# Diagonal sums of the last chunk by VectorE in f32, a last output of 320 and 64 columns, and a new order of steps

## The chip, the cores and the metric

The kernel runs on one core of a Trainium2 chip. The metric is device time in microseconds (us) of one execution; a median of several runs is given, and one further execution was taken with the hardware profiler. The engines have short names: PE is TensorE (matmuls; PEld its weight loads), DVE is VectorE, ACT is ScalarE, POOL is GpSimd, SP is SyncE, which here only issues DMA transfers.

## The reference

An RWKV attention with a decaying state, and after it two matmuls with a squared ReLU between them. Cut to what is computed:

```python
# r, k, v: (4, 8, 768, 48) f32; w, u: (8, 48); w_in (384, 2048), w_out (2048, 384)
for t in range(S):
    cur = einsum('bhd,bhe->bhde', u[None] * k_t, v_t)
    y[:, :, t] = einsum('bhd,bhde->bhe', r_t, state + cur)
    state = w[None, :, :, None] * state + einsum('bhd,bhe->bhde', k_t, v_t)
x = y.transpose(0, 2, 1, 3).reshape(B * S, H * D)       # (3072, 384)
h = maximum(x @ w_in, 0.0)
out = (h * h) @ w_out
```

The part with `u` is the diagonal of the attention: token t sees its own v with the weight sum over d of r, u and k. That sum, for each token and head, is "the diagonal sum" below.

## The kernel before

The 768 tokens are cut into 6 chunks of 128, and each chunk of each of the 4 batches is a unit: 24 units, numbered chunk by chunk, so units 20 to 23 are the last chunk. The heads are padded from 48 to 64 and lie in pairs of 128 rows (`HP` = 4 pairs).

For each unit, in short names that are also the keys of the planner:

- `rt`, `kt` (function `load`, on SP) and `vt` (`load_v`, on POOL) bring r, k and v in f32, 192 KB each.
- `scale` (DVE) multiplies r and k by powers of w and casts to bf16 (`rkw`). `rkT` turns them: units 0 to 5 by PE (`turn`) and ACT, all later ones by a transposing DMA of SP (`turn_dma`).
- `at` (8 matmuls) makes the scores of the 8 heads; `mask` (two DVE products) keeps their upper triangle.
- `rk` (DVE) is the bf16 product of the turned r and k; `sums` multiplies it on PE with `uwb`, a block matrix of u, in 4 matmuls of 8 columns: these are the diagonal sums `t["d"]`. Where a next chunk follows, 4 more matmuls of 96 columns make the step of the state (`sadd`, `sdec` on DVE, `stb` on ACT).
- `dv` (DVE) multiplies the sums with v, `y` (8 or 12 matmuls) applies scores and state to v, and `yb` (DVE) adds the two.
- `xT` turns the result: units 0 to 5 by PE and ACT, the others by a transposing DMA of SP (`x_dma`).
- `m1` (function `mm1`): for each of four quarters of `w_in`, 12 matmuls of 128 columns; `relu` (ACT) and `sq` (ACT or DVE) follow.
- `m2` (`mm2`): for each quarter of `w_out`, 4 matmuls of 384 columns, accumulated over the four quarters; `osb` (ACT) empties the bank and `out` (SP) stores 192 KB.

The last unit's output is made in two parts, `PARTS`, of 256 and 128 columns (`mm2_half`): the first part is emptied by ACT and the second by DVE, and each is stored by itself.

The order of all this is written out by hand for each engine: a class `Plan` simulates the engines with a cost for each step and always starts, on a free engine, the ready step of lowest rank. Each step is added with its engine, cost, needs and rank; the table `TURNS` replaces the ranks of single steps. What comes out is one fixed list per engine, which that engine works through in order: a step that waits holds up all behind it on its engine. Where PE has nothing ready in the first 16 us of the plan, it gets a filler matmul (`fill`, L380).

The eight weight quarters (I 0 to I 3 of w_in, O 0 to O 3 of w_out, 128 x 1536 elements each) are loaded by POOL. `FRONT` names for each a `gate`: a tiny POOL copy out of an r or k tile, so that the transfer starts only when that tile has landed. `load_v` has such a gate too: v of a unit waits for k of the unit before.

Lines the text speaks of: L380 filler, L392 spread of the logarithms of w, L436/L438 loads of r and k, L442 gate, L445 and L448 weights, L460/L458 `scale`, L476 transposing DMA of r and k, L487 turn by PE, L513 `rk`, L521 `at`, L533 `mask`, L541 and L546 the two kinds of `sums`, L563 `sdec`, L576 and L582 `y`, L623 `m1`, L647 `m2`, L663 the last output's matmuls, L675 and L679 its copy and store.

Of the kernel before, what the change touches and what calls it, by code (L numbers as in the profile page):

```python
# [9 lines left out]
F32 = mybir.dt.float32  # L10
BF16 = mybir.dt.bfloat16
AF = mybir.ActivationFunctionType
ALU = mybir.AluOpType
# [153 lines left out]
def kernel(  # L167
# [11 lines left out]
    nc = tc.nc  # L179
    B, H, S, D = r.shape  # L180
    C = 128
# [18 lines left out]
        },  # L200
        "O": {
            0: 76.019, 1: 91.228, 2: 107.535, 3: 7
        },
        "rt": {
            0: -83.003, 1: -66.162, 12: 22.377, 13: 28.231, 14: 28.49, 15: 33.657, 3: -36.29, 5: 1.476, 8: 3.237
        },
        "kt": {
            0: -80.584, 1: -55.486, 10: 19.508, 11: 20.529, 2: -47.443, 6: 2.358
        },
        "at": {  # L210
            0: -3.958, 11: 34.671, 4: -16.745, 7: 10.944
        },
        "mask": {
            (1, 0): -39.238, (10, 0): 33.02, (2, 1): 25.375, (5, 1): 1.515
        },
        "sadd": {
            1: 9.124, 4: 45.244
        },
        "rk": {
            2: 13.012, 7: 14.32, 8: 68.867, 9: -12.042  # L220
        },
        "sums": {
            11: 49.353, 2: -24.778, 8: 5.082
        },
        "dv": {
            2: -26.848, 7: 34.164, 9: -12.993
        },
        "stb": {
            2: -9.741, 4: 57.421
        },  # L230
        "scale": {
            (10, 0): 23.594, (11, 0): -15.371, (3, 0): -29.763, (4, 0): 33.082, (7, 1): 6.517, (8, 1): 4.379
# [5 lines left out]
            3: 5.236, 8: 23.726  # L238
# [8 lines left out]
            (4, 0): -1030.12, 12: 30.174, 4: -16.809  # L247
        },
        "y": {
            11: 43.479, 5: 9.48, 6: 18.808, 9: 29.593  # L250
        },
        "sdec": {
            6: 13.634, 8: 4.888, 9: -24.389
        },
        "yb": {
            6: 3.845
        },
        "sq": {
            (0, 1): 18.299, (0, 2): 50.562, (1, 3): 45.386, (2, 2): 48.536, (3, 2): 52.143, (4, 1): 54.301, (9, 2):
            69.323  # L260
        },
        "m1": {
            (0, 2): -16.746, (1, 0): -1.05, (2, 1): -30.817, (3, 0): 10.204, (4, 2): 48.519, (5, 1): 23.695, (5, 2):
            34.027, (7, 1): 57.358, (8, 3): 44.479, (9, 0): 48.671, (9, 2): 56.936, (9, 3): 69.933
        },
        "relu": {
            (0, 2): 29.056, (1, 3): 26.845, (2, 0): -1.314, (3, 0): 53.81, (7, 1): 50.455
        },
        "m2": {
            (1, 1): 27.683, (1, 2): 12.22, (2, 1): 34.668, (2, 3): 24.074, (3, 0): 21.896, (3, 1): 50.716, (3, 3):  # L270
            -14.219, (4, 0): -2.879, (5, 3): 5.654, (6, 1): 66.17, (7, 1): 43.242, (7, 2): 41.92, (8, 0): 93.885
        },
        "I": {
            0: 0, 1: 1, 2: 3, 3: 5
# [7 lines left out]
    PAIRED = ()  # L282

# [91 lines left out]
    gate = const.tile([128, 1], F32)  # L375

# [133 lines left out]
    def rk(i):  # L510
        t = tiles[i]
        t["rk"] = work.tile([128, HP, C], BF16, name="rk")
        nc.vector.tensor_tensor(t["rk"], t["rkT"][:, 0], t["rkT"][:, 1], ALU.mult)  # L513

# [141 lines left out]
    PARTS = (slice(0, 256), slice(256, dm))  # L656
# [36 lines left out]
    def do(fn, *a):  # L693
        return lambda: fn(*a)
# [19 lines left out]
    for n, (what, q, gated) in enumerate(FRONT):  # L714
        copy(
            (what, q), POOL, 1.0, do(weights, gated, q, what), rank=n,
            move=((2.35, 96, 2.8, 0.0, 0.0) if what == "I" else (2.15, 65, 2.8, 0.0, 0.0)), needs=[gated], uses=[gated],
        )
    for i in range(NU):
# [44 lines left out]
        add(("rk", i), DVE, 0.335, do(rk, i), rank=a + 1, needs=[("rkT", i)], new=[("rk", i)], uses=[("rkT", i)])  # L764
# [9 lines left out]
        for o in range(2):  # L774
# [4 lines left out]
        add(  # L779
            ("sums", i), PE, 0.275 if c < NCH - 1 else 0.105, do(sums, i), rank=a + (2.1 if c else 2.1),  # L780
            needs=[("rk", i), "uwb", ("at", i)] + ([("kb", i) if i < NKE else ("scale", i, 1), ("vb", i)] if c < NCH - 1 else []),
            new=[("s", i)], uses=[("rk", i), ("rkw", i)] + ([vb] if c < NCH - 1 else []),
        )
        add(("dv", i), DVE, 0.465, do(diag_v, i), rank=a + 2, needs=[("sums", i), ("vb", i)], new=[("dv", i)], uses=[("s", i), vb])
# [27 lines left out]
    for m in GROUPS:  # L812
# [17 lines left out]
        for j in range(i, i + m):  # L830
# [12 lines left out]
            for n in range(2):  # L843
                add(
                    ("m2", j, n), PE, (1.74, 0.9)[n], do(mm2_half, j, n), rank=a + n + L2,
# [4 lines left out]
                    ("osb", j, n), (ACT, DVE)[n], 0.3, do(evict_half, j, n), rank=a + n + L2 + 0.4, needs=[("m2", j, n)],  # L850
# [4 lines left out]
        rt=7, kt=7, vt=7, rkw=NPAD, g=2, rkT=6, vb=NVB, rk=4, am=8, dv=4, yb=4, xT=3, gr=6, osb=6,  # L855
# [34 lines left out]
```

## Time and profile before

| | us |
|---|---|
| median of 3 runs | 175.74 (175.08 to 176.27) |
| the profiled execution | 176.04 |
| its span, first to last instruction | 174.3 |
| POOL gate copies in front of v (L465), idle until k landed | 80.9 |
| DVE squares (L640), idle until ACT's relu | 21.5 |
| ACT copies of the output (L654), idle until PE | 15.8 |

The span lies within the profiled execution's own time; 1.7 us are around it. Idle time of an engine that nobody waits for costs nothing: the three largest waits in the table belong to engines that others do not wait for at that moment. In the profile's views, rows of groups end with busy time, mean ns of one instruction, idle time before it and what ended it. Rows in order of time begin with start and length in us.

### The profile page before, as it was taken

To read this page: it belongs to the slowest core of one execution; us is meant where nothing else is said; L and a number is where in the kernel's file an instruction comes from. 1 tells how busy PE (TensorE), PEld (TensorE's weight loads), DVE (VectorE), ACT (ScalarE), POOL (GpSimd) and SP (SyncE) were. 2 spreads that over 40 slices of the span, in tenths; PEclk is the share of its full clock that TensorE was granted. 3 is DMA by queue.
4 is the path that set the end of the run, shared out by engine and by line. 5 is a ranking of instruction groups with operands and counts; after the bars stand their busy time and mean duration, and the time that the engine had idled before them with its cause. 6 is when DMAs were issued, how large, how long until landed. Compare 5 with 4: busy or idle time off the path is not lost.

```text
span 174.3 us, 5795 instructions
## 1 busy us (share of the span) xinstructions
PE 166.7 (96%) x2390; PEld 134.7 (77%) x2390; DVE 121.1 (70%) x252; ACT 132.1 (76%) x268; POOL 40.0 (23%) x84
## 2 busy tenths in 40 slices
PE   7978899999999999999999999999999999999991
PEld 6766799887687787886896787869787698877871
DVE  7869976615999899977986799794989635531010
ACT  3946999999458797886968876939994869948640
POOL 7866890300140220302032202203202000000000
PEclk9999999999999999999999999999999999999999
DMA  4889999999999999999999999999999971130121
GB/s 97 228 179 246 232 218 193 185 221 118 170 201 164 178 154 209 200 214 170 231 142 183 156 237 214 218 177 141 186 200 175 271 180 26 26 111 6 47 81 56
DMA packets 76474, 28.93 MB, mean 166 GB/s; under 512 B 65440, under 2 KB 75296, under 8 KB 76448
## 3 DMA queue, kind: packets, MB, share of 16 engines
q1 hardware_dynamic: 70848, 20.56, 69.8%
q0 software_dynamic: 5312, 7.87, 23.9%
q8 instruction: 18, 0.29, 0.8%
q10 hardware_dynamic: 288, 0.15, 0.4%
q14 instruction: 8, 0.07, 0.1%
HBM read 20.50 MB, written 4.72 MB: 145 GB/s over the span
## 4 chain that ended last, share of the span: by engine, by line
PE 81%; DMA 11%; SPq 4%; issue 1%; DVE 0%; POOL 0%; POOLq 0%
PE bank L623 35%; PE bank L647 33%; DMA w_in_q<-in_moe_w_in_dram 5%; SPq L436 4%; DMA rkT<-rkw 4%; PE bank L521 4%; DMA rt<-in_r_dram 2%; PE bank L576 2%; PE bank L582 2%; PE bank L546 2%; PE bank L663 2%; PE bank L541 1%; PE bank L487 0%; PE bank L607 0%; POOL gate L442 0%
## 5 line engine op out<-in xcount | busy, mean ns | idle before, releaser
L623 PE MATMUL bank<-xT,w_in_q 128*128 128x128 bf16 x1152 | 70.7, 219 | 0.1
L623 PEld LDWEIGHTS <-w_in_q 128*128 128x128 bf16 x1152 | 66.5, 98 | 3.1 <-DMA w_in_q<-in_moe_w_in_dram 0.3
L647 PE MATMUL bank<-w_out_q,g 128*128 128x384 bf16 x368 | 66.9, 326 | 0.0
L631 ACT ACTIVATE gr<-bank 128x512 f32<-128x512 f32 x96 | 54.3, 599 | 13.6 <-PE bank L623 13.3
L647 PEld LDWEIGHTS <-g 128*128 128x128 bf16 x368 | 33.3, 98 | 19.8
L638 ACT ACTIVATE g<-gr 128x512 bf16<-128x512 f32 x72 | 43.7, 637 | 0.4
L533 DVE TENSOR_TENSOR am<-bank,smask 128x512 bf16<-128x512 f32 x48 | 31.3, 682 | 3.3 <-PE bank L521 3.1
L640 DVE TENSOR_TENSOR g<-gr 128x512 bf16<-128x512 f32 x24 | 16.5, 686 | 21.5 <-ACT gr L631 21.5
L465 POOL COPY gate<-kt 128x1 f32<-128x1 f32 x22 | 5.8, 266 | 80.9 <-DMA kt<-in_k_dram 80.9
L654 ACT COPY osb<-bank 128x384 f32<-128x384 f32 x23 | 11.0, 483 | 15.8 <-PE bank L647 15.8
L467 POOL DMA_DIRECT2D vt<-in_v_dram x24 | 21.4, 893 | 5.9 <-issue 1.6
L555 DVE TENSOR_TENSOR dv<-vb,bank 128x384 f32<-128x384 bf16 x24 | 13.2, 548 | 5.3 <-PE bank L546 3.4
L513 DVE TENSOR_TENSOR rk<-rkT 128x512 bf16<-128x512 bf16 x24 | 10.0, 417 | 7.7 <-DMA rkT<-rkw 4.3
L591 DVE TENSOR_TENSOR yb<-bank,dv 128x384 bf16<-128x384 f32 x24 | 13.2, 550 | 2.8 <-PE bank L582 2.4
L471 ACT CAST vb<-vt 128x384 bf16<-128x384 f32 x24 | 12.4, 518 | 0.0
L458 DVE TENSOR_TENSOR rkw<-rt,wpos 128x384 bf16<-128x384 f32 x18 | 9.8, 550 | 1.4 <-DMA rt<-in_r_dram 1.4
L458 DVE TENSOR_TENSOR rkw<-kt,wneg 128x384 bf16<-128x384 f32 x18 | 9.9, 549 | 0.9 <-DMA kt<-in_k_dram 0.9
L567 ACT CAST stb<-st 128x384 bf16<-128x384 f32 x20 | 10.4, 519 | 0.0
L380 PE MATMUL bank<-warm 128*128 128x128 bf16 x98 | 9.3, 248 | 1.1 <-DVE warm L322 1.1
L521 PE MATMUL bank<-rkT 64*128 64x128 bf16 x192 | 9.5, 219 | 0.2
L494 ACT COPY rkT<-bank 128x512 bf16<-128x512 bf16 x12 | 6.8, 588 | 3.0 <-PE bank L487 3.0
L563 DVE TENSOR_TENSOR st<-st,wend 128x384 f32<-128x384 f32 x16 | 8.8, 549 | 0.0
(74 smaller groups left out, 129.1 us busy)
## 6 DMA issues: line engine op xcount, KB each, us to landing
vt<-in_v_dram POOLq DMA_DIRECT2D x24, 192.0 KB, 4.6
out_dram<-osb SPq DMA_DIRECT2D x23, 192.0 KB, 4.0
rt<-in_r_dram SPq DMA_DIRECT2D x18, 192.0 KB, 4.5
kt<-in_k_dram SPq DMA_DIRECT2D x18, 192.0 KB, 4.3
w_in_q<-in_moe_w_in_dram POOLq DMA_DIRECT2D x4, 384.0 KB, 7.9
w_out_q<-in_moe_w_out_dram POOLq DMA_DIRECT2D x4, 384.0 KB, 12.7
kt<-in_k_dram SPq DMA_DIRECT2D x12, 96.0 KB, 4.3
rt<-in_r_dram SPq DMA_DIRECT2D x11, 96.0 KB, 4.2
```

What stands on the lines that cost most here:

```text
L458: nc.vector.tensor_tensor(t["rkw"][:, x, :, :, :D], pair(src), pair(wneg if x else wpos), ALU.mult)
L467: nc.gpsimd.dma_start(out=tiles[i]["vt"], in_=v[b, :, c * C : (c + 1) * C, :].rearrange("h s d -> s h d"))
L471: nc.scalar.copy(tiles[i]["vb"], tiles[i]["vt"])
L521: nc.tensor.matmul(out=t["at"][o][:, p, :], lhsT=t["rkT"][sl, 1, p, :], rhs=t["rkT"][sl, 0, p, :], start=True, stop=True,)
L533: nc.vector.tensor_tensor(am, t["at"][o], smask.unsqueeze(1).to_broadcast([C, HP, C]), ALU.mult)
L555: nc.vector.tensor_tensor(t["dv"], t["vb"], t["d"].unsqueeze(2).to_broadcast([C, H, D]), ALU.mult)
L591: nc.vector.tensor_tensor(t["yb"], t["y"], t["dv"].rearrange("p h d -> p (h d)"), ALU.add)
L623: nc.tensor.matmul(out=t["h", s][:, a], lhsT=turned, rhs=chunks[c]["xT"][:, n, b : b + m, :], start=(n == 0), stop=(n == NK - 1),)
L631: nc.scalar.activation(t["gr", s], t["h", s], AF.Relu)
L638: nc.scalar.activation(g, x, AF.Square)
L640: nc.vector.tensor_tensor(g, x, x, ALU.mult)
L647: nc.tensor.matmul(out=t["o"], lhsT=chunks[units[i][0]]["g"][:, f, units[i][1], :], rhs=w_out_q[f // 4][:, f % 4, :], start=(f == 0), stop ...
```

## The change

Four things are changed.

1. For units 20 to 23 (`NDV = 20`) the diagonal sums no longer come from PE. Three DVE instructions make them from the f32 tiles: r times k, times u, and a reduction over the 48 elements of each head. `dv` then reads them from SBUF. The 4 matmuls of 8 columns of each of these units, and the bf16 product before them, are gone. `r` and `k` tiles are read by these steps too.
2. For this u must lie on all 128 partitions: four f32 matmuls of 96 columns in the head spread it (`spread_u`), and DVE copies it to SBUF (`copy_u`).
3. The last output's parts are 320 and 64 columns wide.
4. `TURNS` and `FRONT` are new, and so is the order on every engine.

```diff
@@ functions
+    u_all = const.tile([C, H, D], F32)
+    def spread_u():
+        spread["u"] = bank("h", "u")[:, :dm]
+        for a in range(HP):
+            nc.tensor.matmul(
+                out=spread["u"][:, a * 2 * D : a * 2 * D + 2 * D], lhsT=ident4[:, a : a + 1].to_broadcast([HP, 128]), rhs=wu[:, 1, :, :D],
+                start=True, stop=True,
+            )
+    def copy_u():
+        nc.vector.tensor_copy(u_all.rearrange("p h d -> p (h d)"), spread["u"])
+    def r_by_k(i):
+        t["rku"] = work.tile([C, H, D], F32, name="dv")
+        nc.vector.tensor_tensor(t["rku"], t["rt"], t["kt"], ALU.mult)
+    def by_u(i):
+        nc.vector.tensor_tensor(x, x, u_all, ALU.mult)
+    def add_heads(i):
+        t["d"] = work.tile([C, H], F32, name="d", bufs=4)
+        nc.vector.tensor_reduce(t["d"], t["rku"], mybir.AxisListType.X, ALU.add)
...
-    PARTS = (slice(0, 256), slice(256, dm))
+    PARTS = (slice(0, 320), slice(320, dm))
@@ the plan
+    add("ucast", PE, 0.35, spread_u, rank=-45, needs=["wu"], new=[("h", "u")])
+    add("uall", DVE, 0.46, copy_u, rank=-20, needs=["ucast"], uses=[("h", "u")])
...
+        if i < NDV:
             add(("rk", i), DVE, 0.335, do(rk, i), ...
+        else:
+            add(("rk", i), DVE, 0.48, do(r_by_k, i), rank=a - 4 + 0.2, ...
+            add(("rku", i), DVE, 0.48, do(by_u, i), rank=a - 2, ...
+            add(("sums", i), DVE, 0.48, do(add_heads, i), rank=a - 1, ...
@@ the order
     FRONT = (
-        ("I", 0, ("kt", 2)), ("I", 1, ("rt", 2)), ("I", 2, ("rt", 4)), ("I", 3, ("kt", 3)),
-        ("O", 3, ("kt", 4)), ("O", 0, ("rt", 3)), ("O", 1, ("rt", 4)), ("O", 2, ("kt", 2)),
+        ("I", 2, ("rt", 4)), ("O", 3, ("kt", 4)), ("O", 0, ("kt", 3)), ("I", 1, ("rt", 2)),
+        ("I", 0, ("kt", 1)), ("I", 3, ("rt", 4)), ("O", 1, ("kt", 2)), ("O", 2, ("kt", 2)),
     )
```

What the new order is, engine by engine, in the places that matter to the text:

- POOL issues the weights as I 0, I 1, O 0, I 2, (v of unit 4), I 3, O 1, O 2, O 3; before it was I 0, I 1, I 3, I 2, (v of unit 4), O 0, O 1, O 2, O 3. v keeps its places.
- PE has 92 fillers instead of 98. In the head, one filler and then the spread of u stand behind the spread of the logarithms, then four fillers and the turn of unit 0; before these were eleven fillers and that turn. After I 1 has landed, PE takes four `m1`, one turn and one `y`, then `m2` of unit 0 with O 0, a block of small steps, `m2` of unit 1, and only then the first `m1` with I 2; I 3 comes five `m1` later. At the first `m2` with O 1 both orders have done the same steps.
- Ahead of `at` of unit 20, PE has `m2` (16, 0) in place of `m2` (15, 3), `sums` 19 and `y` 19; ahead of `at` of unit 21 one `m2` more and `sums` 20 less.
- SP's list is the same until the middle of the kernel. Later k of unit 20 is issued before rkT of 18 (before: after it and two more transposes); ahead of rkT of 20 stand r of 23 and the store of 13 in place of r of 22 and the store of 10; ahead of rkT of 21 stand the stores of 12, 13 and 14 more, and k of 23 less. k of 22 is right before rkT of 21, and k of 23 right after it.
- DVE's list from the scale of k of unit 22 on reads: scale, r by k of 22, a square, by u of 22, `dv` 21, reduction of 22, the two masks of 21. Before, the bf16 product of 21 and the masks of 21 followed the scales of 23.

More of the change, by code (lines that the diff above doesn't have):

```diff
@@ L778 @@
             )
[L779 to L784, printed above, removed]
+        if i < NDV:
+            add(
+                ("sums", i), PE, 0.275 if c < NCH - 1 else 0.105, do(sums, i), rank=a + (2.1 if c else 2.1),
+                needs=[("rk", i), "uwb", ("at", i)] + ([("kb", i) if i < NKE else ("scale", i, 1), ("vb", i)] if c < NCH - 1 else []),
+                new=[("s", i)], uses=[("rk", i), ("rkw", i)] + ([vb] if c < NCH - 1 else []),
+            )
+        add(("dv", i), DVE, 0.465, do(diag_v, i), rank=a + 2, needs=[("sums", i), ("vb", i)], new=[("dv", i)], uses=[("s" if i < NDV else "d", i), vb])
         if c < NCH - 1:
@@ L849 @@
                 add(
[L850 removed]
+                    ("osb", j, n), (ACT, DVE)[n], (0.35, 0.24)[n], do(evict_half, j, n), rank=a + n + L2 + 0.4, needs=[("m2", j, n)],
                     new=[("osb", j, n)], uses=[("o", j, n)],
@@ L854 @@
     room = dict(
-        rt=7, kt=7, vt=7, rkw=NPAD, g=2, rkT=6, vb=NVB, rk=4, am=8, dv=4, yb=4, xT=3, gr=6, osb=6,
+        rt=7, kt=7, d=4, vt=7, rkw=NPAD, g=2, rkT=6, vb=NVB, rk=4, am=8, dv=4, yb=4, xT=3, gr=6, osb=6,
     )
```

70 lines of the change are left out of this document (43 added, 27 removed), and 11 rows, old and new, of the table TURNS.

## The prediction

> **What bounds the kernel now.** I read the page first (busy shares), then the busy time by stretches, then the chain of waits in order of time.
>
> ```profile
> span 174.3 us, 5795 instructions
> ...
> PE 166.7 (96%) x2390; PEld 134.7 (77%) x2390; DVE 121.1 (70%) x252; ACT 132.1 (76%) x268; POOL 40.0 (23%) x84
> ...
> q1 hardware_dynamic: 70848, 20.56, 69.8%
> ...
> out_dram<-osb SPq DMA_DIRECT2D x23, 192.0 KB, 4.0
> ...
> kt<-in_k_dram SPq DMA_DIRECT2D x18, 192.0 KB, 4.3
> ```
>
> ```profile
> 0.00:22.00 22.00, 18.17 (x282) 15.19 (x283) 18.00 (x53) 15.61 (x33) 16.46 (x42) 1.00 0.89 197
> 22.00:130.00 108.00, 107.96 (x1589) 87.41 (x1589) 85.47 (x169) 88.00 (x180) 22.44 (x41) 1.00 1.17 187
> 130.00:138.00 8.00, 7.80 (x107) 5.84 (x101) 6.42 (x14) 5.44 (x13) 1.10 (x2) 1.00 1.16 225
> 138.00:168.00 30.00, 30.00 (x391) 23.86 (x389) 10.94 (x19) 22.17 (x44) 0.00 (x0) 1.00 0.28 70
> 168.00:174.30 6.30, 2.72 (x33) 2.37 (x31) 0.29 (x1) 0.85 (x2) 0.00 (x0) 1.00 0.24 87
> ```
>
> The columns after the stretch are its length, busy time of PE, PEld, DVE, ACT and POOL, the granted clock, the share of the DMA engines, GB/s. From 22 to 168 us PE has matmuls in flight for all but 0.24 us (0.04 + 0.20), so in these 146 us only fewer or shorter matmuls help, and a new wait costs its length. The DMA engines are also full (shares of 1.16 and more, since packets overlap) until about 138 us, and nearly idle after. DVE has only 10.94 of 30 us of work in the last stretch. What is left is the head (22 us) and the tail (6.3 us).
>
> ```profile
> 13.73 8.19 DMA w_in_q<-in_moe_w_in_dram
> ...
> 33.56 1.30 PE bank L647 x8
> 34.86 2.01 PE bank L623 x36
> ...
> 48.03 0.20 PE bank L576 x8
> 48.23 0.17 PE bank L582 x4
> ...
> 97.26 0.08 PE bank L541 x4
> 97.34 0.19 PE bank L546 x4
> ...
> 130.27 6.50 DMA rkT<-rkw
> 136.79 0.44 DVE rk L513
> 137.27 0.26 PE bank L541 x4
> ...
> 168.08 2.65 PE bank L663 x32
> 170.76 0.29 DVE osb L675
> ```
>
> The chain (start, length, what) leaves the DMA once: the quarter I 1 of w_in lands at 13.73 + 8.19 = 21.92 us, and from there PE follows itself. One transfer breaks in, rkT of unit 21, which lands at 130.27 + 6.50 = 136.77 us, just when PE comes to it. The rows also price a step of PE: mm1 of 12 matmuls 2.01/3 = 0.67, mm2 of four 1.30/2 = 0.65, y 0.20 + 0.17 = 0.37, sums 0.08 + 0.19 = 0.27. Adding such prices in PE's order from 21.96 brings y of unit 5 to 47.89; the row says 48.03. So I place steps of the new order by adding prices.
>
> **Part by part.** *The sums.* 16 matmuls of 8 columns (4 units x 4) leave PE in the stretch where it never idles: 4 x 0.08 = 0.33 us; with the full 0.10 that such a group takes beside other steps (four at the 25 ns of the 48-column rows, 0.20/8), 0.40. I take **-0.4**.
>
> ```profile
> L533 DVE TENSOR_TENSOR am<-bank,smask 128x512 bf16<-128x512 f32 x48 | 31.3, 682 | 3.3 <-PE bank L521 3.1
> ...
> L513 DVE TENSOR_TENSOR rk<-rkT 128x512 bf16<-128x512 bf16 x24 | 10.0, 417 | 7.7 <-DMA rkT<-rkw 4.3 <-ACT rkT L494 3.4
> ...
> L563 DVE TENSOR_TENSOR st<-st,wend 128x384 f32<-128x384 f32 x16 | 8.8, 549 | 0.0
> ```
>
> *DVE instead.* Four bf16 products at 417 ns go; eight f32 products of 128x384 come, the same form as the 549 ns row, and four reductions that no row shows, bounded by 417 and twice 549, taken at 549 since they read as many elements. That is 12 x 0.549 - 4 x 0.417 = +4.9 us (4.4 to 7.1). The Trainium skill (VectorE: DVE Perf Modes, "The perf-mode tier table") speaks against this trade: f32 products and all reductions run only at the base rate, and its formula (N+151)/0.96 makes an estimate of 557 ns for 384 elements. The row's 549 agrees for the product; the reduction would by it cost the same, and the sum does not move. Units 20 to 23 get their products before and around 130-145 us, where DVE is busy 6.42 of 8 us and then a third of the time. On PE's path this costs 0 as long as DVE keeps its order; what it queues in front of is in the first rival.
>
> *Weights.* POOL now issues I 0, I 1, O 0, I 2, I 3, O 1, O 2, O 3 (before: I 0, I 1, I 3, I 2, O 0, ...). All weights are of one size, so I give O 0 the slot of I 3, I 3 that of O 0, and I 2 keeps its own.
>
> ```profile
> L445 POOL DMA_DIRECT2D w_in_q<-in_moe_w_in_dram x1: 781/781/781, 17.1 to 17.1; - x1
> ...
> DMA to landing us min/median/max: 7.5/7.5/7.5
> ```
>
> ```profile
> L445 POOL DMA_DIRECT2D w_in_q<-in_moe_w_in_dram x1: 763/763/763, 18.6 to 18.6; - x1
> ...
> DMA to landing us min/median/max: 8.7/8.7/8.7
> ```
>
> The first slot lands at 17.1 + 7.5 = 24.6, the second at 18.6 + 8.7 = 27.3. PE wants O 0 after four mm1, a turn and y, at 25.1: in time. It wants I 2 first after two mm2 (1.30) where it had three mm1 (2.01) ahead of it, 0.7 earlier than before's 27.9, at 27.2: a wait of 0.1, or up to 0.5 if rows of w_out move more slowly than rows of w_in. **+0.1**. I 0 is gated by k of unit 1 and not 2, which lets it go some tenths earlier; I 1 keeps its gate (r of unit 2), and the engines are full, so I 1 stays at 21.9 with 0.3 either way, taken as 0.
>
> *The spread of u in the head.*
>
> ```profile
> 1.06 2.63 PE L380 MATMUL bank<-warm 128*128 128x128 bf16 x23 [1.06 <-DVE warm L322]
> 3.69 0.76 PE L392 MATMUL four<-lnw,ones 32*128 32x96 f32 x8
> 4.38 1.13 PE L380 MATMUL bank<-warm 128*128 128x128 bf16 x11
> ...
> 7.92 1.00 PE L380 MATMUL bank<-warm 128*128 128x128 bf16 x15
> ...
> 13.80 0.62 PE L487 MATMUL bank<-identb,rkw 128*128 128x128 bf16 x8 [1.90 <-DVE rkw L460]
> ```
>
> ```profile
> L330 POOL DMA_DIRECT2D wu<-in_u_dram x1: 606/606/606, 2.3 to 2.3; - x1
> ...
> DMA to landing us min/median/max: 2.5/2.5/2.5
> ```
>
> After the spread of the logarithms and one filler, PE now waits for u, which lands at 2.3 + 2.5 = 4.8, does four f32 matmuls of 96 columns (0.76, by the four of L392) to 5.6, four fillers, and turns unit 0 near 6.0 instead of 5.4. Behind the wait stand fillers and that turn; the copy to SBUF on DVE (about 0.55 by the 549 ns row) falls near the wait for r of unit 1. All this is at most 0.6 late, and at 13.80 PE sat idle 1.90 us for r of unit 2: **0**. Without that cover it would be 0.6.
>
> *SP's order and PE's need, units 20 and 21.*
>
> ```profile
> L476 SPq DMA_TRANSPOSE rkT<-rkw x1: 3837/3837/3837, 122.3 to 122.3; - x1
> ...
> DMA to landing us min/median/max: 7.4/7.4/7.4
> ```
>
> rkT of unit 20 lands at 122.3 + 7.4 = 129.7, and before had no margin there. In the new order PE has one mm2 (0.65) ahead of this unit where it had mm2, sums and y (1.29): it comes 0.64 earlier. SP's queue ahead of that transfer holds as much as before (r of 23 and a store in place of r of 22 and a store), but v of unit 21 is gated by k of 20, which is now loaded well earlier, so one load of 192 KB no longer competes at 119-125 us. A wait between 0 and 0.64; I take **+0.3**. Unit 21: PE comes 0.55 later (one mm2 more, a sums less), and SP has three stores more and one load (k of 23) less ahead of rkT. By bytes (192 KB at 187 GB/s, 1.05) this is +2.1 us; by packets (69.8% of 16 x 174.3 us over 70848 packets, 27.5 ns; 1024 packets to a load of 192-byte rows, 128 to a store: 1.76 against 0.22) it is -1.1. Most packets are the small ones, so I take 0 between: the idle 0.2 of the stretch 130 to 138 goes, and the 0.18 by which the sums after it took longer than others (0.26 against 0.08) go with the sums: **-0.4**.
>
> *The tail.*
>
> ```profile
> 170.26 1.15 SPq L679 DMA_DIRECT2D out_dram<-osb  x2
> ```
>
> 320 and 64 columns instead of 256 and 128: the same 384 in all, and 64 columns at half of 128's cost, so PE ends where it did. The first part ends 64 columns x 16 later (0.44), its store is issued near 170.7, and the second store follows at once: 171.1 as before, with half the bytes. I take 0, between -0.15 and +0.2.
>
> Sum: -0.4 + 0.1 + 0.3 - 0.4 = **-0.4** against the profiled execution, whose 176.04 is the span of 174.3 and 1.7 around it: 175.6. The median of the runs is 0.30 lower, so on that scale 175.74 - 0.4 = **175.3**. The bounds of the unknowns (I 1 0.3 either way; I 2 0 to 0.5; unit 20 0 to 0.64; unit 21 0 to 1.5; tail) give 174.5 to 176.6 for this case.
>
> **The rivals.** *DVE stands behind a late k (slower).* k of units 22 and 23 are now loaded last, k of 22 right before rkT of 21, behind four stores, a load and a transposition more than before. DVE's order is scale 22, product, a square, product, dv 21, sums, and then the two masks that y of unit 21 needs: five at 0.549 and three at 0.682 (the square taken like a mask), 4.8 us. PE wants y of 21 about 3.7 us after at of 21 (five mm2 and the block itself), near 140.8 (137.0 + 3.7). So k of 22 must land by 136.0; each us later costs one. If stores weigh as their bytes, rkT of 21 lands at 138.9 and k of 22 one or two transfers before it, at 136 to 138: +2.0, **177.3**. For it: the 6.50 us of the row at 130.27. Against: the loads it lets pass were heavier in packets.
>
> *The margins open (faster).* If the early v of 21 frees enough, both waits go, I 2 lands in time, and I 1 is 0.3 earlier because I 0 left earlier: -0.4 - 0.4 - 0.3 - 0.15 = -1.2 or a little more, **174.4**.
>
> *The clock in the head.* The rows show fillers at 2.63/23 = 114 ns at 1 us and 1.00/15 = 67 ns at 8 us: PE speeds up on the way. Now six fillers fewer run and PE pauses 0.4 us at 4.4. If the slow pace lasted until 9 us, the 3.4 us from 5.6 on hold at most 51 matmuls at 67 ns, which would take 47 ns more each, 2.4 us; with the 0.6 of the late turn 3.0, of which 1.9 are covered by the idle time at 13.80: +1.1, **176.4**. The Trainium skill (TensorE: Matmul & The Clock Gate, "What's actually happening") has such a rule: the array is at half rate until it was busy through a window of about 3.4 us. The profile's clock column (1.00) does not show the slow pace, the rows do.
>
> *Nothing is gained.* Waits on rkT of 20 and 21 take back what the sums gave: **175.7**.
>
> **Numbers.** Forecast 55%, DVE behind k 15%, margins open 14%, clock 4%, nothing gained 12%. A change under 1% (1.76 us) cannot be told from none here: faster means under 174.0, slower over 177.5. The open margins pass 174.0 in half of their cases, 7%, the forecast in 3%: 0.10 faster; the late k passes 177.5 in half of its cases, 8%, the others in 2%: 0.10 slower; 0.80 the same. The range reaches from under the open margins, 174.0, to the late k, 177.2.
>
> **What would show it.** Right: PE from its first mm1 of I 1 to its last matmul shorter by 0.4 to 0.8, no idle time over 0.5 us at the units 20 to 22, first big mm1 near 21.9. Wrong: PE waiting for masks of unit 21 with DVE idle until k of 22 lands; a wait for w_out q 0 or w_in q 2 between 25 and 28 us; matmuls of over 100 ns after 6 us; the 64-column store landing after 172.6 on the same scale.

## The result, and the profile after

| | before | changed |
|---|---|---|
| median, us (range) | 176.06 (175.08 to 176.84) | 177.14 (176.27 to 178.12) |
| ratio, 95% interval | | 1.0068 (1.0044 to 1.0092) |
| profiled execution | 176.04 | 177.35 |
| its span | 174.3 | 175.2 |
| own time less span, all executions | 1.73 to 1.87 | 2.10 to 2.17 |

Executions over 1.5 per cent above the fastest of the same kernel are left out of every ratio, here and below. The change is slower by 0.7 per cent: 1.2 us by the ratio, 1.1 between the medians. 0.4 us faster was forecast. Of the 1.31 us between the two profiled executions, 0.9 lie in the span and 0.4 outside it. The changed kernel's page and its busy time by stretches (columns as in the prediction):

```profile
span 175.2 us, 5759 instructions
...
PE 169.3 (97%) x2376; PEld 137.3 (78%) x2376; DVE 125.8 (72%) x261; ACT 133.6 (76%) x268; POOL 40.9 (23%) x84
```

```profile
0.00:22.00 22.00, 20.11 (x261) 17.62 (x262) 16.79 (x50) 14.20 (x29) 16.31 (x44) 1.00 0.85 185
22.00:130.00 108.00, 107.71 (x1584) 87.35 (x1582) 87.75 (x173) 89.02 (x181) 23.15 (x41) 1.00 1.12 193
130.00:138.00 8.00, 8.00 (x114) 6.18 (x112) 7.91 (x17) 5.79 (x13) 1.42 (x2) 1.00 0.82 204
138.00:168.00 30.00, 30.00 (x390) 23.66 (x388) 13.10 (x24) 23.65 (x46) 0.00 (x0) 1.00 0.24 59
168.00:175.20 7.20, 3.44 (x37) 2.45 (x35) 0.28 (x2) 0.90 (x2) 0.00 (x0) 1.00 0.24 83
```

PE is busier in the head than before (20.11 against 18.17 us) with fewer matmuls (261 against 282): each takes longer on average. From 130 us to the last output PE never waits. The chain of waits (start, length, what) says where it begins:

```profile
2.30 2.65 DMA wu<-in_u_dram
5.08 1.99 PE bank L436 x8
...
11.13 1.60 PE bank L401 x15
...
23.72 2.01 PE bank L669 x36
...
168.80 2.65 PE bank L709 x32
171.48 0.22 DVE osb L721
```

Before, the chain left the DMA with I 1 at 21.92; now it starts at u, and from 4.95 on PE hardly waits for a transfer. Fifteen fillers take 1.60 us at 11.13, 107 ns each; fifteen took 1.00 at 7.92 before. PE in order of time, changed kernel (an f32 matmul leaves two records, so four are x8):

```profile
3.68 0.76 PE L413 MATMUL four<-lnw,ones 32*128 32x96 f32 x8
4.37 0.29 PE L401 MATMUL bank<-warm 128*128 128x128 bf16 x1
5.08 1.99 PE L436 MATMUL bank<-wu,ident 4*128 4x96 f32 x8 [0.42 <-DMA wu<-in_u_dram]
7.00 0.61 PE L401 MATMUL bank<-warm 128*128 128x128 bf16 x4
7.40 0.63 PE L519 MATMUL bank<-identb,rkw 128*128 128x128 bf16 x4
...
15.32 0.62 PE L519 MATMUL bank<-identb,rkw 128*128 128x128 bf16 x8
...
23.56 1.61 PE L669 MATMUL bank<-xT,w_in_q 128*128 128x128 bf16 x26
```

The same place before:

```profile
5.44 0.40 PE L487 MATMUL bank<-identb,rkw 128*128 128x128 bf16 x4
...
11.47 0.24 PE L541 MATMUL bank<-uwb,rk 128*128 128x8 bf16 x4
...
21.96 2.18 PE L623 MATMUL bank<-xT,w_in_q 128*128 128x128 bf16 x36
```

The turn of unit 0 starts at 7.40 (before 5.44), that of unit 2 at 15.32 (13.80), the first `m1` with I 1 at 23.56 instead of 21.96: the head is **1.60 us late**. From there to the start of the last output's matmuls it is 168.80 - 23.56 = 145.24 us, before 168.08 - 21.96 = 146.12: **0.88 us gained**. The prediction put this down to the sums and the stalls of units 20 and 21; before_with_u below shows that a late head alone brings about half of it. The tail, from the end of the last matmul to the end of the span, grew from 3.54 to 3.73. Together +0.9, the span's difference.

### The profile page after: what moved, and what is told of

Its sections match the earlier page's. It is cut to its first block, busy times and chain, and to the rows that moved or that the text cites. A ratio compares the mean times of both kernels' runs of the same rounds, so it can differ in the third digit from the quotient of the medians.

```text
span 175.2 us, 5759 instructions
## 1 busy us (share of the span) xinstructions
PE 169.3 (97%) x2376; PEld 137.3 (78%) x2376; DVE 125.8 (72%) x261; ACT 133.6 (76%) x268; POOL 40.9 (23%) x84
## 4 chain that ended last, share of the span: by engine, by line
PE 93%; DVE 2%; DMA 2%; issue 1%; POOL 1%; ACT 0%; POOLq 0%
PE bank L669 37%; PE bank L693 35%; PE bank L567 4%; PE bank L401 3%; PE bank L622 3%; PE bank L592 2%; PE bank L628 2%; PE bank L519 2%; PE bank L709 2%; DMA wu<-in_u_dram 2%; PE bank L587 1%; PE bank L436 1%; PE bank L534 1%; PE bank L653 1%; POOL wu L349 0%
## 5 line engine op out<-in xcount | busy, mean ns | idle before, releaser
L669 PE MATMUL bank<-xT,w_in_q 128*128 128x128 bf16 x1152 | 72.0, 219 | 0.0
L693 PE MATMUL bank<-w_out_q,g 128*128 128x384 bf16 x368 | 67.8, 326 | 0.0
L497 POOL COPY gate<-kt 128x1 f32<-128x1 f32 x22 | 7.6, 347 | 82.9 <-DMA kt<-in_k_dram 82.9
L499 POOL DMA_DIRECT2D vt<-in_v_dram x24 | 22.0, 916 | 4.6 <-ACT gr L677 1.6
L601 DVE TENSOR_TENSOR dv<-vb,bank 128x384 f32<-128x384 bf16 x20 | 11.0, 548 | 6.8 <-PE bank L592 6.8
L401 PE MATMUL bank<-warm 128*128 128x128 bf16 x92 | 10.3, 270 | 1.1 <-DVE warm L342 1.1
L545 DVE TENSOR_TENSOR rk<-rkT 128x512 bf16<-128x512 bf16 x20 | 8.4, 418 | 2.9 <-ACT rkT L526 2.2
L605 DVE TENSOR_TENSOR st<-bank,st 128x384 f32<-128x384 f32 x16 | 8.8, 552 | 0.4 <-PE bank L592 0.4
```

The costliest lines, as they stand in the source:

```text
L401: nc.tensor.matmul(out=banks[0][:, :128], lhsT=warm, rhs=warm, start=True, stop=True)
L499: nc.gpsimd.dma_start(out=tiles[i]["vt"], in_=v[b, :, c * C : (c + 1) * C, :].rearrange("h s d -> s h d"))
L669: nc.tensor.matmul(out=t["h", s][:, a], lhsT=turned, rhs=chunks[c]["xT"][:, n, b : b + m, :], start=(n == 0), stop=(n == NK - 1),)
L693: nc.tensor.matmul(out=t["o"], lhsT=chunks[units[i][0]]["g"][:, f, units[i][1], :], rhs=w_out_q[f // 4][:, f % 4, :], start=(f == 0), stop ...
```

## The experiments

Theory at the start: the four matmuls that spread u make the head late, and the rest of the change gains what the middle shows. Rivals: the pause before them or the slow pace behind them makes it late; the new order, the sums on DVE or the parts of 320 and 64 columns cost the time. The table has every kernel that was run several times; "old" and "new" are the orders, "same rows" is the change's way to spread u, "strips" the way of the logarithms of w. The next two columns are from the rows of PE in the profiled execution, the last is the median of own time less span.

| kernel | order, u, sums of 20 to 23 | ratio (95%) | first `m1` with I 1 | last matmul starts | outside the span |
|---|---|---|---|---|---|
| before | old, none, PE | 1 | 21.96 | 170.50 | 1.79 |
| changed | new, same rows, DVE | 1.0068 (1.0044 to 1.0092) | 23.56 | 171.25 | 2.15 |
| changed_again | the same | 1.0076 (1.0047 to 1.0104) | 23.28 | 171.04 | 2.18 |
| before_with_u | old, same rows, PE | 1.0045 (1.0004 to 1.0086) | 23.10 | 171.15 | 1.94 |
| u_filled | new, same rows, no pause | 1.0104 (1.0034 to 1.0174) | 23.89 | - | 2.16 |
| u_gap_256 | new, same rows later, 256/128 | 1.0096 (1.0056 to 1.0135) | 22.96 | 170.62 | 2.16 |
| u_pause | new, late transfer | 1.0020 (0.9971 to 1.0069) | 21.61 | 169.94 | 1.79 |
| u_by_dma | new, late transfer | 1.0018 (0.9974 to 1.0062) | 21.95 | - | 2.19 |
| u_none | new, u left out | 1.0040 (1.0004 to 1.0076) | 21.25 | 170.43 | 2.17 |
| u_rows | new, strips | 1.0019 (0.9994 to 1.0044) | 21.81 | 171.12 | 2.15 |
| u_rows_256 | new, strips, 256/128 | 1.0034 (1.0002 to 1.0065) | 22.60 | 170.88 | 2.19 |
| u_rows_gate | the same, I 2 earlier | 1.0052 (1.0024 to 1.0081) | 22.57 | 170.69 | 2.16 |
| before_sums_dve | old, late transfer, DVE ahead of masks | 1.0060 (1.0035 to 1.0086) | 21.66 | 171.43 | 1.79 |
| before_sums_late | old, strips, DVE behind masks | **0.9950 (0.9922 to 0.9978)** | 22.32 | 170.17 | 1.79 |
| sums_late_u_same | the same with same rows | 1.0059 (1.0030 to 1.0088) | 22.55 | 171.23 | 1.78 |
| before_320_rounds | old, 320/64 | 0.9984 (0.9948 to 1.0020) | 21.11 | 170.53 | 1.80 |
| changed_pad_1 | changed, one DVE memset more | 1.0046 (1.0013 to 1.0079) | 23.42 | 171.10 | 1.79 |

### The spread of u

**u_by_dma**: no spread, no copy; POOL brings u on all partitions while the middle runs.

```diff
-        spread["u"] = bank("h", "u")[:, :dm]
-        for a in range(HP):
-            nc.tensor.matmul(...)
+        pass
 # load_v
+        if i == 9:
+            nc.gpsimd.dma_start(out=u_all, in_=u.unsqueeze(0).to_broadcast([C, H, D]))
```

> The changed kernel, with u brought to all partitions by one late transfer on POOL's queue instead of four matmuls and a copy in the head; all other steps stand in the same order. Theory (the spread of u in the head costs the 1.6 us by which the first mm1 of I 1 starts later, 23.56 against 21.96, and the rest of the change gains 0.85): that mm1 starts near 22.0, the time is 175.3 to 175.9, ratio to before 0.996 to 0.999. Rival (the new order or the DVE sums cost time elsewhere): ratio stays at 1.005 or above.

Without the spread the head is in time again (21.95), with six fillers fewer and with fillers at 107 ns until 10.7. The time is not below before's. In the profiled execution PE waited 1.9 us for one transfer, so its later rows are not used.

**before_with_u**: the kernel before with the spread, its copy and six fillers less; nothing reads the result.

```diff
+        if s["key"] == "fill" and 5 < fills < 12:
+            continue
+        if s["key"] == "fill" and fills == 1:
+            spread_u()
+        if s["key"] == ("scale", 0, 1):
+            copy_u()
```

> The kernel before, with the four f32 matmuls of u, their copy on DVE and six fillers less in the head, placed as in the changed kernel; nothing reads the result. Theory (head alone): the first mm1 of I 1 moves from 21.96 to about 23.5 and the time rises by 1.4 to 1.7, ratio 1.008 to 1.010. Rival (it is the new order of weights and loads that makes the head late): mm1 stays within 0.3 of 21.96, ratio under 1.002.

The spread alone, in the old order:

```profile
5.41 1.99 PE L416 MATMUL bank<-wu,ident 4*128 4x96 f32 x8 [0.66 <-DMA wu<-in_u_dram]
...
23.10 1.61 PE L635 MATMUL bank<-xT,w_in_q 128*128 128x128 bf16 x26
```

The head is 1.14 us late and the time 0.45 per cent up. The spread is a cause by itself. From that `m1` to the last matmul it is 148.05 us here (table), in before 148.54 and in the changed kernel 147.69. So 0.5 us of the middle's gain come with a late head in the old order, without any change of the sums: PE then comes behind transfers that it waited for before (between 130 and 138 us it is busy 8.00 of 8 us, in before 7.80). What is left for the sums and the new order is 0.36.

**u_filled** puts six fillers in front of the spread, so that PE does not stand while u arrives. **u_pause** keeps the wait for u but does one matmul of 4 columns in place of the four, and brings u by the late transfer.

```diff
 # u_filled, in spread_u
+        for n in range(6):
+            fill()
 # u_pause, in spread_u and copy_u
-        for a in range(HP):
-            nc.tensor.matmul(...)
+        nc.tensor.matmul(out=spread["u"][:, :4], lhsT=ident4[:, :1].to_broadcast([HP, 128]), rhs=wu[:, 1, 0, :4], start=True, stop=True)
+        nc.vector.tensor_copy(u_all[:, 0, :4], spread["u"][:, :4])
```

> The changed kernel with six fillers more ahead of the spread of u, so that PE does not idle the 0.42 us until u lands. If the idle time keeps PE's pace slow: matmuls come every 56 ns from about 5.1 us on, the four matmuls of u take about 1 us, and the time falls by 1.0 to 1.5 against the changed kernel (ratio to before 0.998 to 1.001). If the long f32 matmuls on four rows keep the pace slow: 107 ns until about 12 us as in the changed kernel, the time within 0.5 of it (ratio 1.004 to 1.010).

> The changed kernel with one f32 matmul of 4 columns in place of the four of 96, at the same place and after the same wait for u; u itself comes by the late transfer. If the idle time of 0.42 us keeps the pace slow: 107 ns until 9 to 12 us, and the first mm1 of I 1 is still 0.8 or more late (ratio 1.002 or above). If the length of the f32 matmuls does it: 56 ns before 6 us, mm1 of I 1 near 22.0, ratio 0.996 to 0.999.

With PE kept busy while u arrives the head is later still (23.89; four executions). Without the long matmuls it is in time (21.61), although fillers run at 107 ns until 9.5. In that execution u came early and PE waited only about 0.1 us for it; u_rows below waits 0.34 and is in time too. So neither the wait nor the slow pace alone makes the head late: the idle time at unit 2 covers them. It takes the length of the spread on top.

**u_rows**: u goes over the array like the logarithms, on four strips of 32 rows.

```diff
+    nc.gpsimd.dma_start(out=urow, in_=u.rearrange("(a o) d -> a (o d)", o=2).unsqueeze(0).to_broadcast([32, HP, 2 * D]))
...
         for a in range(HP):
-            nc.tensor.matmul(...)
+            sl = slice(a * 32, a * 32 + 32)
+            nc.tensor.matmul(out=four[:, a, 2 * D : 4 * D], lhsT=ones[sl], rhs=urow[sl], start=True, stop=True)
```

> The changed kernel with u in four strips of 32 rows, as the logarithms of w are, so that the four f32 matmuls of u lie on different rows of the array. Theory (the prediction's 0.76 was the price of four matmuls side by side on four strips; on the same four rows they run one after another): the four take about 0.7 us and not 1.99, the first mm1 of I 1 falls from 23.56 to 22.0 to 22.6, ratio 0.998 to 1.003. Rival (f32 matmuls cost 2 us wherever they lie): 1.7 us or more, ratio 1.005 or above.

The rows of one line (durations min/median/max in ns, then first and last start), changed kernel:

```profile
L436 PE MATMUL bank<-wu,ident x8: 416/416/495, 5.1 to 6.7; 4*128 4x96 f32 x8
```

and with strips:

```profile
L439 PE MATMUL four<-urow,ones x8: 416/469/523, 5.0 to 5.4; 32*128 32x96 f32 x8
```

Eight matmul records of about the same length: on the same four rows they start over 1.6 us, one after another; on four strips over 0.4 us, side by side. The whole takes 1.99 us in the one and 0.76 in the other, both with fillers at 107 ns around them. Head at 21.81.

**u_gap_256** moves the spread (same rows) to the idle time in front of the turn of unit 2, puts the fillers back and the parts to 256 and 128. On DVE the copy of u now stands ahead of the scale of r of unit 2, which that turn needs.

```diff
+        if s["key"] == "ucast":
+            for n in range(6):
+                fill()
+            continue
...
+        if s["key"] == ("scale", 2, 0):
+            held = s
+            continue
+        if s["key"] == ("turn", 2, 0):
+            spread_u()
+            copy_u()
+            held["emit"]()
```

> The changed kernel with the spread of u moved from 5 us to the place before the turn of unit 2, where PE idles for r, with the eleven fillers of before in the old place, and with the last output as 256 and 128 columns again. Theory (the head's 1.6 us are the spread's place, the tail's 0.2 the first store's later issue, the rest gains 0.85): pace of 56 ns from about 5.2 us, first mm1 of I 1 at 21.9 to 22.2, last matmul near 169.7, ratio to before 0.993 to 0.997. Rival (the new order pays in waits on late transfers what the sums gain): ratio 0.999 or above, with idle PE of 0.5 us or more between 45 and 140 us.

```profile
11.76 1.13 PE L436 MATMUL bank<-wu,ident 4*128 4x96 f32 x8
14.01 0.62 PE L519 MATMUL bank<-identb,rkw 128*128 128x128 bf16 x8 [1.12 <-DVE rkw L492]
...
14.73 1.07 PE L401 MATMUL bank<-warm 128*128 128x128 bf16 x9
```

Fillers run at 56 ns from 4.6 on, and here the four take 1.13 us, not 1.99: part of their length is the pace. Strips at that pace took 0.48, in u_rows_gate (below):

```profile
5.59 0.48 PE L439 MATMUL four<-urow,ones 32*128 32x96 f32 x8 [0.66 <-DMA urow<-in_u_dram]
```

So the same rows cost 2.4 to 2.6 times the strips at either pace. Behind the spread PE waits 1.12 us for the scale that the copy of u held up, and then fillers are back at 107 ns, from 14.7 to 18.2. The turn of unit 2 is 0.2 us later than before (14.01), the first `m1` with I 1 1.0.

### The sums on DVE, the parts, the order

**before_sums_dve**: the old order with the sums of units 20 to 23 by DVE in the place of `rk`, u by the late transfer. **before_sums_late**: the same, but the three instructions stand in `diag_v`, behind the unit's masks, and u comes on strips in the head.

```diff
 # before_sums_dve: in rk(i); before_sums_late: as here
     def diag_v(i):
         t = tiles[i]
+        if i >= 20:
+            x = work.tile([C, H, D], F32, name="dv")
+            nc.vector.tensor_tensor(x, t["rt"], t["kt"], ALU.mult)
+            nc.vector.tensor_tensor(x, x, u_all, ALU.mult)
+            t["d"] = work.tile([C, H], F32, name="d", bufs=4)
+            nc.vector.tensor_reduce(t["d"], x, mybir.AxisListType.X, ALU.add)
```

> The kernel before in its own order, with the diagonal sums of units 20 to 23 by the three DVE instructions and without the 16 matmuls; u comes by one late transfer. Theory: from the first mm1 of I 1 to the last matmul 0.4 us less than before (148.1 against 148.5), the waits at units 20 and 21 remain; ratio 0.996 to 1.000. Rival (the DVE work delays masks): a longer stretch, ratio over 1.002.

> The kernel before, its order kept, with the sums of units 20 to 23 by DVE, but queued behind the masks of their unit instead of ahead of them (where the earlier kernel with sums ahead had PE wait 1.1 us near 133 for a mask), and u spread by four matmuls on four strips of 32 rows in the head, no late transfer. Theory (the waits at 57 and 133 came from the late transfer and from the sums ahead of the masks; without them the 16 matmuls are a gain): head 21.5 to 22.0, no wait of over 0.5 us near 57 or 133, from the first mm1 with I 1 to the last matmul 148.0, ratio 0.996 to 0.999. Rival (DVE's sums delay yb of unit 20 or 21 wherever they stand): a wait of 0.5 to 1 us on a square of unit 20 or on xT behind yb, ratio 1.000 to 1.005.

DVE in before_sums_dve, and PE at the same place:

```profile
130.88 0.55 DVE L517 TENSOR_TENSOR dv<-rt,kt 128x384 f32<-128x384 f32 x1
131.46 0.56 DVE L518 TENSOR_TENSOR dv<-dv,u_all 128x384 f32<-128x384 f32 x1
132.06 0.55 DVE L520 TENSOR_REDUCE d<-dv 128x8 f32<-128x384 f32 x1
132.52 0.68 DVE L543 TENSOR_TENSOR am<-bank,smask 128x512 bf16<-128x512 f32 x1
```

```profile
134.46 0.27 PE L588 MATMUL bank<-vb,am 128*128 128x48 bf16 x4 [0.93 <-DVE am L543]
```

The masks stand behind the three and PE waits 0.93 us for the second. In before_sums_late DVE does the masks first, at the same time:

```profile
130.55 0.68 DVE L546 TENSOR_TENSOR am<-bank,smask 128x512 bf16<-128x512 f32 x1
...
132.35 0.55 DVE L571 TENSOR_TENSOR dv<-rt,kt 128x384 f32<-128x384 f32 x1
```

That wait is gone, and so is one of 0.63 for a turned unit near 57. This kernel is 0.5 per cent **faster** than before by the ratio (the medians alone, 175.41 against 176.00, give 0.3), and its slowest execution (176.39) is faster than all but one of the changed kernel's first thirteen. So in this order the sums on DVE are a gain, behind the masks and with u on strips. The two kernels differ in the way u comes too, so the place of the sums is not shown to be worth all of the 1.1 per cent between them; the trace shows 0.93 us for it.

**sums_late_u_same** turns only the spread back to the same rows (`lhsT=ident4[:, a : a + 1]...`, `rhs=wu[:, 1, :, :D]`, as in the change); **changed_again** is the changed kernel beside it, with no edit.

> The kernel that kept the order of before and had the sums of units 20 to 23 on DVE behind the masks (ratio 0.995), with one thing turned back: u is spread as in the changed kernel, four matmuls on the same four rows, instead of on four strips of 32 rows. Theory (the spread on the same rows makes the head late by 0.8 to 1.3 us and nothing gives it back): first mm1 with I 1 at 23.0 to 23.5, ratio 0.999 to 1.003. Rival (a late head lets waits behind it vanish, as in the new order, so that most of it comes back): ratio 0.995 to 0.997.

> The changed kernel once more, on the chip and beside the runs of before that the two other kernels of this call share. Theory: ratio 1.005 to 1.009 as the first time; against the kernel that keeps the order, with the same spread of u and sums on DVE, 0.4 to 0.6 per cent slower, which is what the new order costs. Rival (the new order costs nothing and u all): within 0.002 of that kernel.

In the old order the way u is spread is worth 1.1 per cent, 0.995 against 1.0059, intervals apart (0.9 by the medians, 175.41 and 177.05). The profiled execution shows it only in part: the head is late by 0.2 us against the kernel with strips, and a wait of 0.76 us for a turned unit stands near 93, which that kernel does not have. Against the changed kernel the old order with the same u and sums is 0.2 per cent better, not the 0.4 to 0.6 expected.

**u_none** (no u at all; the diagonal of units 20 to 23 is left out), **u_rows_256** (strips, 256/128) and **u_rows_gate** (the same, with I 2 waiting for k of 3 instead of r of 4) ask what the new order loses when its head is in time.

```diff
 # u_none
+        nc.vector.memset(u_all, 0.0)
 # u_rows_256
-    PARTS = (slice(0, 320), slice(320, dm))
+    PARTS = (slice(0, 256), slice(256, dm))
 # u_rows_gate
+        if s["key"] == ("I", 2):
+            weights(("kt", 3), 2, "I")
+            continue
```

> The changed kernel with u left out: no spread of u, u_all set to zero by DVE, no late transfer (so the diagonal of units 20 to 23 is left out). This is the rest of the change by itself, with neither the matmuls in the head nor an extra transfer. Theory (the rest gains at most 0.4 us of sums once the head is in time, because PE then comes earlier to transfers that were covered by the late head: I 2 near 27, xT near 82 and 141): first mm1 with I 1 near 21.7, from there to the last matmul 148.0 to 148.6, ratio 0.997 to 1.002. Rival (the late transfer of u in the earlier kernels was what took the gain): from there to the last matmul 147.7 as in the changed kernel, no wait over 0.4 us, ratio 0.993 to 0.996.

> The changed kernel with u on four strips of 32 rows in the head and the last output as 256 and 128 columns as before. Theory (tail shorter by 0.1 to 0.2 us, all else as in the kernel with strips): ratio 0.999 to 1.002, tail 3.5 to 3.6 us. Rival (parts make no difference): ratio as with 320 and 64, 1.002, tail 3.7.

> The kernel with strips and 256/128 columns in the new order (ratio 1.0034), in which I 2 alone waits for k of unit 3 instead of r of unit 4 before it is issued; nothing else moves. Theory (the new order's own loss begins with I 2, which lands at 27.4 to 28.0 whatever the head does, and PE comes to it 0.2 to 0.4 us too early): I 2 is issued near 17.0 instead of 18.3 and lands near 27, the wait at 27.7 goes, ratio 0.0005 to 0.002 lower, that is 1.001 to 1.003. Rival (the engines are full, so I 2 lands when it did and the others later): I 2 at 27.8 or later, the wait stays, ratio 1.003 to 1.005.

All three stay above 1. Only u_none has its head in time (21.25); in the other two it is 0.6 late (22.60 and 22.57), with waits of 0.3 us for scaled tiles near 14 and 16 us. Where PE comes early, it meets transfers. From PE's rows in u_none (waits, with total, times, longest), then PE in u_rows and in u_pause:

```profile
PE bank L688 <- DMA w_out_q<-in_moe_w_out_dram: 1.0, 1, 1.0
...
PE bank L664 <- DMA w_in_q<-in_moe_w_in_dram: 0.2, 1, 0.2
```

```profile
27.42 0.79 PE L669 MATMUL bank<-xT,w_in_q 128*128 128x128 bf16 x11 [0.21 <-DMA w_in_q<-in_moe_w_in_dram]
...
142.45 1.22 PE L669 MATMUL bank<-xT,w_in_q 128*128 128x128 bf16 x19 [0.73 <-DMA xT<-yb]
```

```profile
82.27 0.83 PE L669 MATMUL bank<-xT,w_in_q 128*128 128x128 bf16 x12 [0.47 <-DMA xT<-yb]
```

O 0, I 2 and the turned outputs `xT`: none of these waits is in the changed kernel, whose PE comes later. In the table the last matmul of the new order starts between 169.9 and 171.3 wherever the head ended between 21.25 and 23.56. I 2 alone is not it: gated earlier it was issued 2.1 us sooner than in u_rows_256 (16.59 against 18.73) and landed at 27.4 instead of 28.0, its wait went, and the time did not fall. What costs the medians of these kernels most stays open: the profiled executions of u_rows_256 and u_rows_gate show no wait for `xT` or O 0 and are above before too.

**before_320** (one execution) and **before_320_rounds** change only the parts, `slice(0, 320), slice(320, dm)`.

> The kernel before with the last output as 320 and 64 columns, nothing else. Theory: from the end of the last matmul to the end of the span 3.75 us (3.55 before), since the second store is issued later behind the first. Rival: no difference, 3.5 to 3.6.

> The kernel before with a last output of 320 and 64 columns and nothing else. Theory (the first part ends later by 64 columns times 16 and its store with it, the tail is 0.1 to 0.2 us longer): ratio 1.000 to 1.001. Rival (the shorter second part helps): ratio 0.997 to 0.999. If the one look at 175.02 was typical, 0.994.

175.02 the first time, then 176.31 with 0.9984 (0.9948 to 1.0020): no difference can be told. The tail is 3.62 to 3.64 instead of 3.54. In the new order it is 3.73 with these parts and 3.61 with 256 and 128 (u_rows_256), so the parts are 0.1 of the changed kernel's 0.2.

### The time outside the span

Every execution has its own time and its span. The difference is 1.73 to 1.87 in the kernels of the old order (1.88 to 2.06 in before_with_u), and 2.08 to 2.21 in every kernel of the new order but one, u_pause, at 1.75 to 1.87. u_pause has one DVE record more, 318 instead of 317. **pad_1** and **pad_10** add one and ten memsets to u_rows_256, **changed_pad_1** adds one to the changed kernel:

```diff
+        nc.vector.memset(pad, 0.0)
```

> The changed kernel with u on four strips and 256/128 columns, plus one DVE memset of a scratch column in the head, which nothing reads. Asked is the time of the execution that lies outside its span: 1.78 to 1.80 us in the kernels that keep the order of before (1.91 in one) and in one of the new order that has one more DVE instruction, 2.13 to 2.18 in the nine others of the new order. Theory (it goes with the number of DVE instructions, 317 records in all kernels with the longer time, 318 and more in the others): 1.80 now. Rival (it goes with something else of the new program): 2.13 to 2.18.

> The same with ten such memsets, so that DVE has as many records as in the kernel that keeps the order and has the sums behind the masks. Theory (number of DVE instructions): time outside the span 1.80. Rival: 2.13 to 2.18.

> The changed kernel itself plus one DVE memset of a scratch column behind the copy of u, read by nothing. In the kernel with strips one such memset brought the time outside the span from 2.17 to 1.77 us. Theory (the changed kernel's own 2.14 to 2.18 us outside its span go the same way): 1.77 to 1.80 outside the span, nothing else moves, ratio 0.002 lower than the 1.0068 and 1.0076 measured for it, 1.004 to 1.006. Rival (it was the strips' kernel alone): 2.14 to 2.18 and 1.006 to 1.008.

Outside the span were 1.80 (pad_1, 175.70), 1.79 (pad_10) and, in the twelve executions of changed_pad_1, 1.74 to 1.82. That kernel's ratio fell to 1.0046, as expected, with a span (175.0) like the changed kernel's (medians 175.0 and 175.1). In pad_10's one execution, 177.39, PE waited 1.22 us for `xT` near 84:

```profile
84.14 0.83 PE L672 MATMUL bank<-xT,w_in_q 128*128 128x128 bf16 x12 [1.22 <-DMA xT<-yb]
```

So 0.36 us of the change's 1.2 are not in any row of the profile, and one instruction that does nothing takes them away. It is not simply a count from 318 on, since before_with_u has 319 records and lies between. Without them the changed kernel (1.0046) is no slower than the old order with the same u and sums (sums_late_u_same, 1.0059; intervals overlap). The kernels with strips in the new order carry them too: the median span of u_rows is 174.1 us, that of before beside it 174.2, so its 1.0019 lies outside the span. In u_rows_256 (174.65 against 174.1) and u_rows_gate (174.85 against 174.0) the span is longer as well.

## Why the prediction was wrong

**The step that failed is "The spread of u in the head": 0.** It was priced at 0.76 "by the four of L392", at most 0.6 late, and covered by the 1.90 us at 13.80. It took 1.99 us, and PE's first turn came 2.0 us late instead of 0.6. The four of L392 lie on four strips of 32 rows (operand 32*128) and run side by side; u's lie all on the same four rows (4*128) and run one after another. The row's form said so, and the estimate went by count and columns alone. (The plan that made the new order had put the spread at 0.35.) The Trainium skill (TensorE: Matmul & The Clock Gate, "Part 3: Packing small matmuls — row/col tiling") says that small matmuls run concurrently when they are put on different strips of rows; the two rows of u_rows and the changed kernel agree, 0.76 against 1.99.

The same term also put the slow pace behind the spread at nothing. From the turn of unit 0 to that of unit 2 the same steps took 1.89 us longer than before (7.40 to 15.32 against 5.44 to 11.47). The cover was 2.33 (11.47 to 13.80: the 1.90 idle and two groups of unit 1 that the new order does behind that turn). So 1.96 + 1.89 - 2.33 = 1.52 us late at unit 2, and 1.60 at I 1. With strips, in u_rows, it is 0.67 + 1.34 - 2.33: in time (turns at 6.11 and 13.48).

The rival "the clock in the head" saw the slow pace, at 4 per cent, until 9; it lasted to 12.7 in the changed kernel, and it is harmless without the long spread (u_pause). The section of the Trainium skill that the prediction named there says that the array speeds up after a busy window of some 3.4 us. Two slow spells agree, 8.0 to 11.4 in u_rows_gate and 14.7 to 18.2 in u_gap_256. But in the changed kernel 107 ns stood for over 11 us, with PE idle 0.42 us in it; in u_filled PE was idle 0.28 us ahead of 3.96 and not after, and the slow pace still lasted to 13.0. So a rule by time busy alone would not give it, and what besides counts no run here shows.

**The second term that failed is "1.7 around it"**, carried over unchanged: it became 2.15. Nothing in the profile of before could have told that.

The other steps:

- *The sums, -0.4, and unit 21, -0.4*: right in size; the middle is 0.88 shorter. But before_with_u loses the stalls by its late head alone, so unit 21's part is not shown to be due to the new order; the 0.36 us against before_with_u fit the sums. Unit 20's wait of 0.3 did not come: PE has 8.00 of 8 us between 130 and 138.
- *DVE instead*: the reduction, which no row had shown, takes 0.55 (row of L520), as estimated. That it costs 0 "as long as DVE keeps its order" holds in the changed kernel; in the old order, ahead of the masks, it cost 0.93.
- *Weights, +0.1 with 0 to 0.5*: hidden by the late head in the changed kernel; 0.2 for I 2 in u_rows and u_none, and 1.0 for O 0 in u_none, where O 0 was called in time. The waits for `xT` near 82 and 142, 0.5 to 1.2, were not in the sum at all. They are one reason why a head in time does not bring the new order below before; the 0.36 outside the span is another.
- *The tail, 0 with -0.15 to +0.2*: +0.2, the end of its bounds; not told from nothing by the times.
- *DVE behind a late k* did not occur: with 7.91 of 8 us busy between 130 and 138 DVE had its k, and PE did not wait.
- *The margins open* occurred at unit 21: rkT was issued at 129.78, landed 3.8 later, and PE came to it at 138.61, 5.0 us behind. Its gain went under in the head.
- *The bounds*: the upper one, 176.6, leaves out the 1.5 of unit 21; all the bounds named add up to 178.0. And the measured 177.14 lies within the range that was stated, 174.0 to 177.2, by luck: its top came from the late k, which did not occur.

Sum as measured: head +1.6, middle -0.9, tail +0.2, outside the span +0.4: +1.3 between the profiled executions. What the way of spreading u is worth depends on the order: 1.1 per cent in the old one, 0.3 to 0.5 in the new one (u_rows, u_rows_256), where intervals touch or overlap.

## What to carry to other kernels

Take a matmul's price from a row with the same rows of the array, not only the same count and columns: four f32 matmuls on the same four rows cost 1.99 us, on four strips 0.76, at the same slow pace. A delay in front of a PE-bound stretch is free only up to the idle time that covers it, and a gain behind it counts only if the transfers were not just in time. Work given to DVE belongs behind the masks PE waits for: in the old order the kernel with the sums there was 0.3 to 0.5 per cent faster than before, and ahead of the masks they made PE wait 0.93 us.

## What was not expected of the hardware

- Four f32 matmuls of 96 columns on the same four rows took 1.99 us with fillers at 107 ns around them and 1.13 behind fillers at 56 ns (u_gap_256); on four strips 0.76 and 0.48 (u_rows, u_rows_gate).
- Own time less span was 2.10 to 2.21 us in the changed kernel (both sets of runs) and 1.74 to 1.82 with one more DVE memset. What the 0.36 us are, no row shows.
- The pace changed from 107 to 56 ns per filler at 4.4 to 6.3 us in seven profiled executions (the four of before and its 320/64 and sums_dve variants, u_none, u_gap_256, u_rows_gate) and at 9.5 to 13.0 in the thirteen others; every kernel with the spread on the same rows near 5 us is among these, but so is u_by_dma (10.7), which has no spread. The clock column of the changed kernel shows 1.00 all the while.
- The slow pace can come back: in u_rows_gate at 8.0, behind a wait of 0.31 us, and in u_gap_256 at 14.7, behind the spread and a wait of 1.12. In before it did not after 1.90 us idle at 13.80. Which of these counts was not tested.
